# Turning the plain-head probabilities of batches 2 and 3 by transposing DMAs, in a fused windowed attention and two-layer MLP kernel

## The chip, the cores and the metric

The kernel runs on one core of one Trainium2 chip. The metric is the device time in microseconds (us) of one execution, taken as the median of several runs. Lower is better.

## The reference, cut to what matters

The inputs `q`, `k`, `v` are 8 batches x 8 heads x 576 positions x 64 features in float32. Heads 0 to 3 ("plain") look at the last 32 positions; heads 4 to 7 ("dilated", or "strided") look at every fourth of the last 128 positions. The attention result, seen as 4608 rows of 512, goes through a two-layer MLP with a SiLU between the layers.

```python
scores = scale * np.matmul(q, k.transpose(0, 1, 3, 2))
rel = pos[:, None] - pos[None, :]
mask_plain = (rel >= 0) & (rel < window)                                   # window = 32, heads 0..3
mask_dil = (rel >= 0) & (rel < window * dilation) & (rel % dilation == 0)  # dilation = 4, heads 4..7
scores = np.where(masks[None], scores, -1000000000.0)
scores = scores - np.max(scores, axis=-1, keepdims=True)
attn = np.exp(scores)
attn = attn / (np.sum(attn, axis=-1, keepdims=True) + 1e-09)
attn_out = np.matmul(attn, v)                 # 8 x 8 x 576 x 64
x = attn_out.transpose(0, 2, 1, 3).reshape(4608, 512)
h = x @ w_in                                  # 512 -> 2048
out = (h * (1.0 / (1.0 + np.exp(-h)))) @ w_out    # 2048 -> 512
```

## The kernel before, in words

The kernel works batch by batch. For each batch b there are 16 steps of layer one (`layer1`, one step for each of 16 groups of 128 hidden features; eight matmuls on TensorE and one SiLU on ScalarE a step) and then layer two (`layer2`, 16 or 20 steps of four matmuls of 128x512; every four steps end one tile of output rows, which VectorE copies out of PSUM and SyncE's queue stores). While TensorE does the MLP of batch b, the attention of the batches b+1 and b+2 is put between its steps. Nothing is scheduled automatically: the order of each engine's instructions is the order in which the Python code issues them. `plan_of(b)` writes a table from step numbers to calls (`at(step, function, ...)`), and `plan(s)` issues the calls of step s just ahead of that step's matmuls. Steps 0 to 15 belong to layer one, steps 16 and up to layer two; in layer two of batch 1 the steps run to 35.

The attention of one batch b comes in two halves, z = 0 (plain heads) and z = 1 (strided heads), each half in two parts hi = 0, 1, and each part goes through the same chain:

- `load_rows(b)` (lines 123 to 144) or `load_qk(b)`: GpSimd's queue loads q and k into a tile `nat`; `load_v(b)` loads v into `vw`, and `shift_*` copy parts of `vw` to other partitions.
- `cross(b, z)` (lines 146 to 159): two transposing DMAs on SyncE's queue for each half, out of `nat` into the tile `plain` (z = 0, line 152) or `strided` (z = 1, lines 158 and 159). Batch 3 is the first that is transposed so; batches 1 and 2 use TensorE (`transpose`).
- `scores(b, z)`: TensorE computes blocks of scores, VectorE adds the mask and takes maxima. `exps(b, z, hi)`: ScalarE's exponentials, with the sums.
- `normal(b, z, hi)` (lines 565 to 578): VectorE takes reciprocals of the sums and writes the normalised probabilities `pn` in float16, 8 or 10 blocks of 64 columns.
- The probabilities then have to be transposed, from `pn` to a tile `ptT`, which can be done in two ways. `turn` (line 585) lets TensorE transpose 4 or 5 blocks of 128x128 a part into PSUM, and `turned` (line 593) lets VectorE or ScalarE copy them to SBUF. `turn_by_dma` (lines 595 to 602) issues one transposing DMA on SyncE's queue, SBUF to SBUF, and needs neither TensorE nor the copy.
- `values(b, z)` (lines 627 and 691): TensorE multiplies by v. `finish(b, z, copies)` (lines 704, 696, 698): the copies of the result out of PSUM into `xT`, the input of layer one, by VectorE alone or, with `both`, half by VectorE and half by ScalarE.

In the kernel before, batches 0 to 2 and the plain half of batch 3 are turned by TensorE; the strided half of batch 3 and all of batches 4 to 7 by DMA. The helper `later` issues normalisation, turn, values and finish for batch 2 (both halves, in layer two of batch 1) and for the plain half of batch 3 (in layer one of batch 2, steps 0, 4 and 6).

SyncE's queue is in order: an instruction that waits holds up what stands behind it. In layer two of batch 1 it holds, in this order: the first two output tiles' stores, the third store, `cross(4, 0)` and `cross(4, 1)` at step 28, and the fourth and fifth store. GpSimd's queue holds the loads of batch 4 (`load_rows(4)`, from step 17), and at step 0 of batch 2 `load_v(4)` and the strided rows of batch 5, which start once `values(2, 1)` has set the old `vw` free.

PSUM has two tiles of the pool `big` for the matmuls of the MLP and four tiles of the pool `ps`, which scores, turns and values use in turn. `pn` and `ptT` have four buffers each.

Of the kernel before, what the change touches and what calls it, by code (L numbers as in the profile page):

```python
# [29 lines left out]
def kernel(  # L30
# [9 lines left out]
    nc = tc.nc  # L40
# [754 lines left out]
    def transposes(at, b, z, step):  # L795
        for which in (1, 0):
            at(step, transpose, b, z, which, both)

    def later(at, b, z, steps, copies=(nc.vector.tensor_copy, nc.vector.tensor_copy)):

        for hi in (0, 1):
            if steps[hi] is not None:
                at(steps[hi], normal, b, z, hi)
        for hi in (0, 1):
            at(steps[2], turn, b, z, hi)
        for hi in (0, 1):
            at(steps[2], turned, b, z, hi, copies[hi])
        at(steps[3], values, b, z)
        at(steps[3], finish, b, z, copies)

    def plan_of(b):
        ev = {}

        def at(s, fn, *args):
            ev.setdefault(s, []).append((fn, args))

        def all_exps(b, z):
            for hi in (0, 1):
                at(16, exps, b, z, hi)

        if b == 0:

            at(-16, normal, 0, 1, 1)
            at(-15, shift_class, 0, dve, 1, 2)
            at(-14, normal, 0, 0, 1)
            at(-8, turn, 0, 1, 1)
            at(-8, turned, 0, 1, 1, act)
            at(-4, turn, 0, 0, 1)
            at(-4, turned, 0, 0, 1)
            at(-4, values0, 1, 1)  # L830
            at(-4, last_values, 0, 1, (1,))
            at(-4, finish0, 1, 1)
            at(-4, last_finish, 0, 1, 1)
            at(-2, values0, 0, 1)
            at(-2, last_values, 0, 0, (1,))
            at(-2, finish0, 0, 1, both)
            at(-2, last_finish, 0, 0, 1)
            at(-2, clear_short, 1, nc.vector)
            at(-2, load_v, 1)
            for c in (2, 3):  # L840
                at(-2, load_w_out, c)
            at(-2, load_qk, 2)
            transposes(at, 1, 1, 2)
            at(8, scores, 1, 1)
            for hi in (0, 1):
                at(8, shift, 1, 1, hi)
            for which in (1, 0):
                at(18, transpose, 1, 0, which, (dve, dve) if which else (act, act))
            at(20, normal, 1, 1, 0)
            at(20, scores, 1, 0)  # L850
            at(14, shift_v, 1, nc.sync.dma_start)
            at(18, load_rows, 3)
            at(18, load_v, 2)
            all_exps(1, 1)
            for hi in (0, 1):
                at(20, exps, 1, 0, hi)
            for n, z, hi in ((20, 1, 1), (26, 0, 0), (28, 0, 1)):
                at(n, normal, 1, z, hi)
            for n, z, copies in ((27, 1, (dve, dve)), (30, 0, both)):
                for hi in (0, 1):  # L860
                    at(n, turn, 1, z, hi)
                for hi in (0, 1):
                    at(n, turned, 1, z, hi, copies[hi])
                at(n + 1 + z, values, 1, z)
                at(n + 1 + z, finish, 1, z, both)
        elif b == 1:
            transposes(at, 2, 0, 3)
            transposes(at, 2, 1, 11)
            at(2, shift_v, 2, nc.sync.dma_start)
            for z in (0, 1):  # L870
                at(2, cross, 3, z)
                at(28, cross, 4, z)
            at(9, scores, 2, 0)
            for hi in (0, 1):
                at(12, shift, 2, 0, hi)
            at(17, load_v, 3)
            at(17, nc.gpsimd.tensor_copy, latch, qTs[1][:, 1, S - 1 : S])
            at(17, load_rows, 4)
            at(14, scores, 2, 1)
            all_exps(2, 0)  # L880
            all_exps(2, 1)
            for hi in (0, 1):
                at(19, normal, 2, 0, hi)
            at(21, scores, 3, 0)
            at(21, exps, 3, 0, 0)
            at(21, exps, 3, 0, 1)
            later(at, 2, 0, (None, None, 27, 28))
            later(at, 2, 1, (29, 31, 33, 34))
        else:
            if b + 2 < B:  # L890
                at(0, load_v, b + 2)
                if b + 3 < B:
                    at(0, load_rows, b + 3, (1, 0))
                if b + 3 < B:
                    at(12, cross, b + 3, 0)
                if b > 2:
                    at(12, cross, b + 2, 1)
            if b + 1 < B:
                at(1 if b == 2 else 0, shift_plain, b + 1, dve, 0, NM)
                at(12, shift_class, b + 1, dve, 0, 2)  # L900
                at(12, shift_over, b + 1, dve)
                if b == 2:
                    later(at, 3, 0, (0, 0, 4, 6))
                else:
                    at(6, values, b + 1, 0)
                    at(6, finish, b + 1, 0)
                x = {2: 13, 3: 12}.get(b, 11)
                at(x, scores, b + 1, 1)
                at(x, shift, b + 1, 1, 1)
                all_exps(b + 1, 1)  # L910
            if b + 2 < B:
                at(18 if b == 2 else 17, scores, b + 2, 0)
                for hi in (0, 1):
                    at(18, exps, b + 2, 0, hi)
            if b + 1 < B:
                for hi in (0, 1):
                    at(22 + hi, normal, b + 1, 1, hi)
                    at(22 + hi, turn_by_dma, b + 1, 1, hi)
                at(29, values, b + 1, 1)
                at(29, finish, b + 1, 1)  # L920
            if b + 2 < B:
                for hi in (0, 1):
                    at(27 + hi, normal, b + 2, 0, hi)
                    at(27 + hi, turn_by_dma, b + 2, 0, hi)

        def plan(s):
            for fn, args in ev.pop(s, ()):
                fn(*args)

        return plan  # L930
# [49 lines left out]
    for b in range(B):  # L980
        plan = plan_of(b)
        if b == 0:
            for x in range(NFF):
                plan(2 * x - NFF)
                plan(2 * x + 1 - NFF)
                layer1_part(2 * x % NFF, 2 * x // NFF, first[x] if x < 4 else None)
        else:
            for f in range(NFF):
                plan(f)
                layer1(b, f)  # L990
        if b == 0:
            layer2_first(plan)
        else:
            layer2(b, plan)
        for s in range(NFF, 3 * NFF):
            plan(s)
# [30 lines left out]
```

## Time and profile before

| what | value |
|---|---|
| time before, median of 3 runs | 308.5 us (307.78 to 308.84) |
| the profiled execution: its time | 307.98 us |
| the profiled execution: span of its instructions | 306.1 us |
| granted TensorE clock, mean | 0.989 |
| TensorE (PE) busy | 294.8 us, 96% |
| VectorE (DVE) busy | 178.2 us, 58% |
| ScalarE (ACT) busy | 187.5 us, 61% |
| TensorE transposes of probabilities, `turn`, plain half of batch 2 | 9 in 0.50 us, at 88.39 us |
| the same, plain half of batch 3 | 9 in 0.50 us, at 102.81 us |
| transposing DMAs of probabilities (18 in the run), issue to landing | 2.4 / 2.6 / 7.9 us (least, median, most) |

PE is TensorE's matmuls, DVE VectorE, ACT ScalarE, POOL GpSimd, SP SyncE; a name with a q (SPq, POOLq) is that engine's instruction queue, which issues DMAs. Times of instructions are microseconds from the start of the span. A line number with L is a line of the kernel. The profiled execution takes 1.88 us more than its span (307.98 against 306.1), and is itself 0.52 us below the median of the runs.

### The profile page before, as it was taken

Reading aid. Unit: us, or ns where it says so; the run is one execution under the profiler, and the core shown is the slowest. Engines: PE = TensorE matmul, PEld = TensorE weight load, DVE = VectorE, ACT = ScalarE, POOL = GpSimd, SP = SyncE. Lnnn points to the kernel's source line nnn. Section 1 sums busy time; section 2 is a strip of 40 time slices with the busy share of each in tenths; the row PEclk is TensorE's granted clock in tenths of the full one; section 3 lists DMA queues with packets and bytes.
Section 4 is the critical chain, followed back from the end, with each engine's and each line's share of the span. In section 5 each row is a group of like instructions: output and inputs, shape, how many; then the busy total and the mean of one; then the engine's idle time right before and its main releaser. Section 6 shows DMA issues by size and latency. Waiting matters only on the chain.

```text
span 306.1 us, 10365 instructions
## 1 busy us (share of the span) xinstructions
PE 294.8 (96%) x4466; PEld 189.2 (62%) x4466; DVE 178.2 (58%) x370; ACT 187.5 (61%) x556; POOL 92.3 (30%) x139
## 2 busy tenths in 40 slices
PE   5689999999999999999999999999999999999995
PEld 2557754677555875477644775467644775477544
DVE  6896579518797738943785447842885344620011
ACT  2676677676894559945792558945793558246200
POOL 8634544962473831086007610040000000000000
PEclk9689999999999999999999999999999999999999
DMA  8999999999999999599889995494035000400022
GB/s 106 179 213 203 174 197 218 170 197 182 164 156 191 170 189 103 135 141 176 108 154 176 194 113 105 130 177 82 4 77 144 36 2 12 135 36 2 9 94 71
DMA packets 104878, 39.21 MB, mean 128 GB/s; under 512 B 79568, under 2 KB 100048, under 8 KB 104832
## 3 DMA queue, kind: packets, MB, share of 16 engines
q0 software_dynamic: 63104, 18.88, 62.6%
q1 hardware_dynamic: 41584, 19.60, 30.3%
q8 instruction: 35, 0.57, 0.8%
q14 instruction: 11, 0.09, 0.1%
q10 hardware_dynamic: 144, 0.07, 0.1%
HBM read 37.75 MB, written 9.44 MB: 154 GB/s over the span
## 4 chain that ended last, share of the span: by engine, by line
PE 87%; DMA 7%; ACT 2%; DVE 1%; issue 1%; POOL 1%; POOLq 0%; SPq 0%
PE h L717 36%; PE o L782 33%; PE o L756 5%; PE h L737 4%; DMA w_in<-in_moe_w_in_dram 4%; PE x L627 3%; DMA nat<-in_q_dram 2%; PE s L379 1%; PE s L391 1%; ACT pe L560 1%; PE t L329 1%; PE pt L585 1%; DMA ptT<-pn 1%; POOL nat L168 1%; PE xs L691 1%
## 5 line engine op out<-in xcount | busy, mean ns | idle before, releaser
L725 ACT ACTIVATE gT<-h 128x576 f16<-128x576 f32 x112 | 72.9, 651 | 77.5 <-PE h L717 77.3
L782 PE MATMUL o<-w_out,gT 128*128 128x512 f16 (+1 forms) x528 | 114.1, 373 | 0.0
L717 PE MATMUL h<-xT,w_in 128*128 128x288 f16 x896 | 113.5, 286 | 0.0
L717 PEld LDWEIGHTS <-w_in 128*128 128x128 f16 x896 | 86.4, 98 | 23.3 <-DVE xT L704 0.3
L782 PEld LDWEIGHTS <-gT 128*128 128x128 f16 x528 | 50.7, 98 | 54.9
L560 ACT ACTIVATE pe<-ms,nm 128x64 f32<-128x64 f32 x178 | 59.1, 333 | 2.8 <-DVE nm L528 2.7
L766 DVE COPY ob<-o 128x512 f32<-128x512 f32 (+1 forms) x34 | 23.1, 681 | 45.9 <-PE o L782 44.9
L512 DVE SCALAR_TENSOR_TENSOR ms<-s,mask 128x512 f32<-128x512 f32 x28 | 19.2, 686 | 35.7 <-PE s L391 24.7
L560 ACT ACTIVATION_READ_ACCUMULATOR pe<-ms,nm 128x1 f32 x178 | 33.2, 187 | 0.0
L704 DVE CAST xT<-x 128x512 f16<-128x512 f32 x26 | 16.8, 685 | 21.2 <-PE xs L691 21.2
L177 POOL DMA_DIRECT2D vw<-in_v_dram x16 | 10.1, 634 | 61.4 <-PE xs L691 59.2
L576 DVE TENSOR_TENSOR pn<-pe,r 128x640 f16<-128x640 f32 (+2 forms) x32 | 25.3, 792 | 1.1
L528 DVE TENSOR_REDUCE nm<-ms 128x10 f32<-128x640 f32 (+1 forms) x28 | 22.0, 787 | 1.0
L737 PE MATMUL h<-xT,w_in 128*128 128x256 f16 (+1 forms) x128 | 16.9, 286 | 1.6 <-issue 0.9
L134 POOL DMA_DIRECT2D nat<-in_k_dram x20 | 15.2, 764 | 6.7 <-DMA vw<-in_v_dram 6.0
L134 POOL DMA_DIRECT2D nat<-in_q_dram x20 | 14.6, 749 | 6.3 <-DMA nat<-in_k_dram 4.0
L756 PE MATMUL o<-w_out,gT 128*128 128x512 f16 x64 | 15.2, 379 | 0.2 <-issue 0.2
L737 PEld LDWEIGHTS <-w_in 128*128 128x128 f16 x128 | 11.9, 98 | 5.4 <-issue 1.9
L744 ACT ACTIVATE gT<-h 128x512 f16<-128x512 f32 (+1 forms) x16 | 10.1, 652 | 6.3 <-PE h L737 6.1
L627 PEld LDWEIGHTS <-vw 64*64 64x64 f16 x896 | 8.4, 108 | 5.2 <-issue 5.2
L766 ACT COPY ob_last<-o 128x128 f32<-128x128 f32 x1 | 0.3, 266 | 17.0 <-DVE ob_last L766 17.0
L569 DVE TENSOR_REDUCE l<-pe 128x10 f32<-128x640 f32 (+2 forms) x12 | 9.6, 801 | 1.5 <-ACT pe L551 1.4
(101 smaller groups left out, 257.7 us busy)
## 6 DMA issues: line engine op xcount, KB each, us to landing
out_dram<-ob SPq DMA_DIRECT2D x35, 256.0 KB, 2.5
vw<-in_v_dram POOLq DMA_DIRECT2D x8, 288.0 KB, 8.4
vw<-in_v_dram POOLq DMA_DIRECT2D x16, 128.0 KB, 5.6
w_in<-in_moe_w_in_dram POOLq DMA_DIRECT2D x4, 512.0 KB, 12.5
w_out<-in_moe_w_out_dram POOLq DMA_DIRECT2D x4, 512.0 KB, 11.2
nat<-in_k_dram POOLq DMA_DIRECT2D x6, 256.0 KB, 6.8
nat<-in_q_dram POOLq DMA_DIRECT2D x6, 256.0 KB, 8.2
nat<-in_k_dram POOLq DMA_DIRECT2D x20, 72.0 KB, 7.1
```

The source lines that it names most:

```text
L134: nc.gpsimd.dma_start(out=f[:, 2 * (1 - which) + h // 2, 0 : ZR - 1, h % 2], in_=src[b, h].rearrange("(m p) d -> p m d", p=RT),)
L512: nc.vector.scalar_tensor_tensor(out=ms[:, 0:8].rearrange("p (n t) c -> p n (t c)", n=2), in0=s[hi].rearrange("p n t c -> p n (t c)"), sca ...
L528: nc.vector.tensor_reduce(out=nm[:, 0:w], in_=ms[:, 0:w], axis=AX.X, op=ALU.max, negate=True)
L560: nc.scalar.activation(pe[:, t, :], slot(t), AF.Exp, scale=1.0 if b else scale, bias=nm[:, t : t + 1], accum_out=l[:, t : t + 1],)
L576: nc.vector.tensor_tensor(pn[:, 0:w], a["pe", z, hi][:, 0:w], r[:, 0:w, None].broadcast_to([P, w, KB]), ALU.mult)
L627: nc.tensor.matmul(dst, w, p, start=True, stop=True)
L717: nc.tensor.matmul(h[:, half, 0:HS], w_in16[:, c, f * P : f * P + P], xT[:, c, half * HS : half * HS + HS], start=(c == 0), stop=(c == MC ...
L725: nc.scalar.activation(gT[:, f, s0 : s0 + S].rearrange("p (a c) -> p a c", a=2), h[:, :, 0:HS], AF.Silu)
L737: nc.tensor.matmul(h[:, i, 0 : c1 - c0], w_in16[:, c, (f + i) * P : (f + i + 1) * P], xT[:, c, c0:c1], start=(c == 0), stop=(c == MC - 1),)
L756: nc.tensor.matmul(o, gT[:, f, t * P : (t + 1) * P], w_out16[:, f, :], start=(f == 0), stop=(f == NFF - 1),)
L766: copy(ob, o)
L782: nc.tensor.matmul(o, gT[:, f, t * P : (t + 1) * P], w_out16[:, f, m0:m1], start=(f == 0), stop=(f == NFF - 1),)
```

## The change

The plain halves of batches 2 and 3 are turned by `turn_by_dma` and no longer by `turn` and `turned`. For batch 2 the DMAs are issued at step 19 of batch 1, right behind each part's `normal`. For batch 3 the normalisation moves from step 0 of batch 2 to step 34 of batch 1, where its two parts stand on VectorE's queue before and after the `finish` of batch 2's strided half, and each is followed by its DMA. That `finish` is now shared by VectorE and ScalarE (`both`). `values` and `finish` keep their steps (28 of batch 1 and 6 of batch 2). `cross(4, 1)` moves from step 28 to step 35, behind batch 3's two new DMAs on SyncE's queue; `cross(4, 0)` stays at step 28. The helper `later` goes; its other calls are written out at the steps that they had.

```diff
@@ in plan_of, b == 1
             at(2, shift_v, 2, nc.sync.dma_start)
             for z in (0, 1):
                 at(2, cross, 3, z)
-                at(28, cross, 4, z)
+            at(28, cross, 4, 0)
             at(9, scores, 2, 0)
...
             for hi in (0, 1):
                 at(19, normal, 2, 0, hi)
+                at(19, turn_by_dma, 2, 0, hi)
             at(21, scores, 3, 0)
             at(21, exps, 3, 0, 0)
             at(21, exps, 3, 0, 1)
-            later(at, 2, 0, (None, None, 27, 28))
-            later(at, 2, 1, (29, 31, 33, 34))
+            at(28, values, 2, 0)
+            at(28, finish, 2, 0)
+            for hi in (0, 1):
+                at(29 + 2 * hi, normal, 2, 1, hi)
+                at(33, turn, 2, 1, hi)
+            for hi in (0, 1):
+                at(33, turned, 2, 1, hi)
+            at(34, values, 2, 1)
+            at(34, normal, 3, 0, 0)
+            at(34, turn_by_dma, 3, 0, 0)
+            at(34, finish, 2, 1, both)
+            at(34, normal, 3, 0, 1)
+            at(34, turn_by_dma, 3, 0, 1)
+            at(35, cross, 4, 1)
@@ in plan_of, b >= 2
-                if b == 2:
-                    later(at, 3, 0, (0, 0, 4, 6))
-                else:
-                    at(6, values, b + 1, 0)
-                    at(6, finish, b + 1, 0)
+                at(6, values, b + 1, 0)
+                at(6, finish, b + 1, 0)
```

More of the change, by code (lines that the diff above doesn't have):

```diff
@@ L797, in transposes @@
             at(step, transpose, b, z, which, both)
[L799 to L809, printed above, removed]
     def plan_of(b):
```

## The prediction

> **What bounds the kernel now.** I read the page first, then the chain of waits in order of time, then SyncE's and VectorE's timelines around the edit, last the landings of single DMAs.
>
> The page says that TensorE is busy for 96% of the span, and that the chain that ended last lies on it for 87%:
>
> ```profile
> PE 294.8 (96%) x4466; PEld 189.2 (62%) x4466; DVE 178.2 (58%) x370; ACT 187.5 (61%) x556; POOL 92.3 (30%) x139
> PE 87%; DMA 7%; ACT 2%; DVE 1%; issue 1%; POOL 1%; POOLq 0%; SPq 0%
> ```
>
> The chain in order of time (start, length, what) shows how the edited stretch lies on it:
>
> ```profile
> 88.39 0.50 PE pt L585 x9
> 88.89 0.86 PE o L782 x4
> 89.75 0.61 PE x L627 x64
> ...
> 102.81 0.50 PE pt L585 x9
> 103.31 1.96 PE h L717 x16
> 105.27 0.61 PE x L627 x64
> ```
>
> Each piece begins where the last one ends, so TensorE has no idle time here. The two groups of L585 are the transposes that go; the two groups of L627 are the `values` that must then wait for a DMA. SyncE's queue in the same stretch, with the line at which the DMAs of batch 3 stand in its order:
>
> ```profile
> 77.35 3.86 SPq L158 DMA_TRANSPOSE strided<-nat  x1
> 81.31 2.14 SPq L159 DMA_TRANSPOSE strided<-nat  x1
> 85.31 5.53 SPq L767 DMA_DIRECT2D out_dram<-ob  x3
> 91.07 6.24 SPq L152 DMA_TRANSPOSE plain<-nat  x2
> 97.49 3.42 SPq L158 DMA_TRANSPOSE strided<-nat  x1
> 101.01 1.18 SPq L159 DMA_TRANSPOSE strided<-nat  x1
> ```
>
> The queue is free from 83.45 to 85.31, where the DMAs of batch 2 will be issued. It is held by `cross(4, 0)` from 91.07 to 97.31, and the DMAs of batch 3 stand behind that. VectorE writes the probabilities of batch 2's second part, and those of batch 3, here:
>
> ```profile
> 83.85 0.82 DVE L576 TENSOR_TENSOR pn<-pe,r 128x640 f16<-128x640 f32 x1
> ...
> 99.97 0.69 DVE L576 TENSOR_TENSOR pn<-pe,r 128x512 f16<-128x512 f32 x1
> ...
> 101.03 0.83 DVE L576 TENSOR_TENSOR pn<-pe,r 128x640 f16<-128x640 f32 x1
> ```
>
> The last view is the landing of a transposing DMA of probabilities: all 18 of them (least, median, most), and then the one issued at 163.0 alone:
>
> ```profile
> DMA to landing us min/median/max: 2.4/2.6/7.9
> ...
> DMA to landing us min/median/max: 5.6/5.6/5.6
> ```
>
> The second is issued 0.7 us after GpSimd begins to load v and rows for a later batch (162.30); the same place in two other batches gives 7.9 (issued at 130.12, loads from 129.45) and 5.8 (199.24, loads from 198.57). Without such loads it is 2.4 to 2.7, once 3.2 and once 3.3. That spread decides this case.
>
> **What goes from TensorE.** Twice nine transposes, 0.50 us each time by the chain, 56 ns a transpose. TensorE has no gap on either side, so what goes from it shortens the chain: 1.00 us in all. No other matmul goes, so this is the most that the change can give. [...] The chain's 56 ns decide, and I take 1.00.
>
> **What goes from VectorE.** Two pairs of copies out of PSUM, 0.81 us at 88.76 and 0.80 at 103.36. VectorE is not on the chain here, so I count nothing for them; they make it earlier by 0.81 before `finish` of batch 2.
>
> **Batch 2's two DMAs, step 19.** The first part's `pn` is written by 82.6, the queue is free at 83.45, and an issue takes 1.2 us (the least of the 18): 83.5 to 84.7. The second part's `pn` ends at 84.67, so its DMA is issued at 84.8 and done issuing at 86.0. `values(2, 0)` comes at 89.75 less the 0.50 that has gone, 89.25. That leaves 4.45 us for the landing. The nearest row is the store that SyncE issues at 85.31 in the same traffic; it landed after 2.7 us, and the q and k rows that GpSimd issues between 81.4 and 86 landed after 3.0 to 3.5. By those the data are there at 87.5 to 88.3, and nothing waits. The far ends are 2.4 and 7.9, so the wait lies between nothing and 3.45 us; I take nothing. The first store is pushed from 85.31 to 86.1; its buffer is one of five and nobody waits for it.
>
> **Batch 3's normalisation, step 34.** Its instructions cost VectorE 1.05 us (part 0, from 99.54 to 100.6) and 1.28 us (part 1, to 101.9) as before; what moves is their place. The copies after the turn of batch 2's strided half end at 96.06 less 0.5, so part 0 runs to 96.6, while TensorE is still in `values(2, 1)` (which ends at 97.06 less 0.5). VectorE's half of `finish`, half of the 1.55 us that it now takes alone from 96.99 to 98.54, runs to 97.4; ScalarE, idle from 95.2 to 99.9, does the other half at the same time. Layer one of batch 2 reads `xT` from 98.4 on: nothing waits. Part 1 then runs to 98.7, and behind it stands the copy of the last output tile, which frees the PSUM buffer that the second step of layer one needs at 99.4. It now ends at 99.62 and would end at 98.7 + 0.69 = 99.4. So between nothing and 0.2 us are lost; I take nothing.
>
> **Batch 3's two DMAs.** Ahead of them on SyncE's queue stand `cross(4, 0)`, to 97.3 (0.5 earlier if its start moves with TensorE, at 96.8), and a store of 0.3 to 0.5 us. So the first is issued at about 97.7 and the second, whose `pn` is there at 98.7, at about 99.0. `values(3, 0)` comes at 105.27 less 1.00, 104.27. That leaves 5.3 us. GpSimd's loads begin at 96.97 less 0.5, ahead of both. By the quiet rows (2.6) the data are there at 101.6; by the loaded rows at 104.6 (5.6), 104.8 (5.8) and 106.9 (7.9): a wait between nothing and 2.6 us. The rows that have SyncE's own traffic of this very stretch are a strided transpose issued at 97.49, which landed after 8.7 us but moves over three times the data, and stores at 102.28 and 102.75 with 6.8 and 8.0, which stood behind both strided transposes. In the changed order those come after the turns. So I take a landing below the loaded rows, 3 to 5 us, and no wait, but only by 0.3 to 2.3 us.
>
> **`cross(4, 1)` moved to step 35.** Two issues, 3.42 and 1.18 us, move from 97.49 to about 100.3, and the fifth store behind them from 102.75 to about 105.5. The strided scores of batch 4 are needed in layer one of batch 3, after 144 us; the next thing on the queue is `cross(5, 0)` at 115.29. It costs nothing, and the cover is some 10 us.
>
> **Sum.** Profiled execution 307.98, less 0.50, less 0.50, and nothing added: 306.98. It lies 0.52 below the median of the runs (308.5), so the same 1.00 off the median gives 307.5 us, 0.32% less. A measurement of this kernel can tell about 0.3%, 0.93 us, from no change, so even the full gain hardly clears that.
>
> **The rivals.**
>
> *Late batch 3 (slower).* The two new DMAs are issued behind `cross(4, 0)` and in the middle of GpSimd's loads, and `values(3, 0)` holds all of TensorE's queue until the second one lands. If `cross(4, 0)` ends a microsecond later, because batch 2's turns have slowed the rows that it transposes, the second DMA is issued at 100; with 7.9 us it lands at 107.9, 3.6 us late. With 7.9 alone it is 2.6 late. Taking 2.8 in the middle, 308.5 - 1.0 + 2.8 = 310.3 us. It decides from a landing of 5.3 us on, and makes the kernel slower by more than 0.3% from about 7.2. For it: three of three turns issued beside GpSimd's loads took 5.6 to 7.9. Against it: those loads come in bursts, and the DMA is at 1.20 of its share from 96 to 104 us against 1.24 from 163 to 169. [...]
>
> *Short wait.* The same wait, but of 0.3 to 1.5 us (landing 5.6 to 6.8): most of the gain is given back, 307.8 to 309.0, middle 308.3. No change that can be measured.
>
> *Late batch 2.* The second turn of batch 2 takes 5.4 us, like the store issued at 88.87, or up to 7.9: it lands at 90.2 to 92.7 against 89.25, 1.0 to 3.4 us late, and the time is 308.5 to 310.9. Against it are the rows of 2.7 and 3.5 from the same moment.
>
> That the change does not do what it says can be excluded: both `turn`s are TensorE instructions, and they are gone.
>
> **How the numbers follow.** In time 0.42, short wait 0.18, late batch 3 0.28, late batch 2 0.12. In time gives 307.5, itself 306.9 to 308.0 by the spread of the runs. Of its 0.42, I put 0.32 at more than 0.3% faster, and 0.10 within, as the gain is so near the bound. Short wait is within. Of late batch 2 half is within and half slower, late batch 3 is slower: faster 0.32, same 0.34, slower 0.34. The range goes from 306.9 to the middle of the late case, 310.3; beyond it is about half of that case.
>
> **What would show it.** L585 must have 18 matmuls fewer and L600 four DMAs more. In time: in the chain, L627 near 89.2 and 104.3 follows L782 and L717 with no gap, and both DMAs of each pair have landed before. Short wait or late: TensorE's loads of weights show an idle time before L627 put down to `ptT`, in the first or the second place, and the landing of the turn just ahead of it is over 4.4 or 5.3 us. Wrong altogether: a new wait of TensorE in any other place, or a gain over 1.1 us, since I see only 1.00 on the chain.

## The result and the profile after

The changed kernel takes 316.49 us (median of 4 runs, 315.91 to 317.72) against 308.67 us before (4 runs): a ratio of 1.0256, 95% interval 1.0233 to 1.0279. The forecast was 307.5 us, with a range to 310.3. The profiled execution takes 315.91 us; its span of 313.4 us is 7.3 us longer than before. Ratios, here and below, are of the fast runs alone and medians of all runs, so where a kernel had a slow run (three of the versions below) its median lies above what its ratio says.

The page after. Eighteen matmuls fewer, and still TensorE's share of the span falls; in the chain by lines the transposing DMAs of probabilities rise from 1% to 5%. In the row of the granted clock, the 15th of 40 slices shows a 6. The profile of before has a 6 and an 8 in that row too, but in its second and third slice, at the start of the kernel; so the mean of 0.989 is the same in both profiles and shows nothing of it:

```profile
PE 298.5 (95%) x4448; PEld 191.3 (61%) x4448; DVE 177.4 (57%) x364; ACT 188.1 (60%) x558; POOL 91.7 (29%) x139
...
PEclk9999999999999969999999999999999999999999
...
PE h L717 35%; PE o L782 31%; DMA ptT<-pn 5%; PE h L737 5%; PE o L756 5%; PE x L627 3%; DMA nat<-in_q_dram 2%; PE s L391 2%; PE s L379 2%; ACT pe L560 1%; PE pt L585 1%; PE t L329 1%; PE xs L691 1%; POOL nat L168 1%; DVE pn L576 1%
```

The chain of waits in order of time (start, length, what) shows both places. Where the transposes stood, the chain now leaves TensorE, goes through a DMA, and comes back at `values` (L627):

```profile
84.96 5.06 DMA ptT<-pn
90.02 0.04 issue
90.06 0.68 PE x L627 x63
...
99.27 1.11 PE h L717 x10
100.38 9.13 DMA ptT<-pn
109.51 0.04 issue
109.56 1.04 PE x L627 x32
110.59 0.11 PE xs L691 x4
110.70 9.13 PE h L717 x56
```

The last line matters too: the 56 matmuls of layer one behind the second wait take 9.13 us; before they took 6.97, as these lines of the chain before show:

```profile
90.43 4.42 PE o L782 x20
...
105.95 6.97 PE h L717 x56
112.92 0.61 PE s L391 x64
```

The stretches of 2 us around the wait (busy time of PE first, then PEld, DVE, ACT, POOL; granted clock, DMA share and GB/s last) show TensorE idle, and then at half its clock:

```profile
106.00:108.00 2.00, 0.00 (x0) 0.00 (x0) 0.00 (x0) 0.00 (x0) 0.69 (x1) 1.00 1.75 153
108.00:110.00 2.00, 0.45 (x33) 0.44 (x36) 0.00 (x0) 0.00 (x0) 0.00 (x0) 0.57 1.37 133
110.00:112.00 2.00, 2.00 (x60) 1.48 (x53) 1.40 (x4) 0.00 (x0) 0.72 (x1) 0.50 1.36 179
112.00:114.00 2.00, 2.00 (x11) 1.25 (x9) 1.25 (x4) 0.65 (x1) 0.67 (x1) 0.50 1.57 161
114.00:116.00 2.00, 2.00 (x14) 1.42 (x13) 0.00 (x0) 0.70 (x2) 0.91 (x3) 0.73 1.95 145
```

SyncE's queue after. The four new DMAs (L600) are issued where they were expected, within 1.4 us; it is their landing that is late:

```profile
82.90 3.26 SPq L600 DMA_TRANSPOSE ptT<-pn  x2
86.25 4.00 SPq L767 DMA_DIRECT2D out_dram<-ob  x3
90.49 6.89 SPq L152 DMA_TRANSPOSE plain<-nat  x2
97.47 0.54 SPq L767 DMA_DIRECT2D out_dram<-ob  x1
98.11 3.57 SPq L600 DMA_TRANSPOSE ptT<-pn  x2
101.85 7.63 SPq L158 DMA_TRANSPOSE strided<-nat  x1
```

The ledger (what each place adds to the span) comes from comparing the starts of the same work in the two chains. At 82.3 the changed kernel is 0.10 us ahead. The 20 matmuls behind `values(2, 0)` start at 90.81, 0.38 later than before, though 0.50 of transposes are gone: a wait of 0.98. The 56 behind `values(3, 0)` start at 110.70, 4.75 later, with another 0.50 gone: 4.87 lost. Of these TensorE is idle for 0.48 and 3.76; the other 0.63 are the products themselves, which are split by the wait and run at the lower clock. The scores behind those start 6.91 later (119.83 for 112.92): 2.16 more, the slow matmuls. To the end of the chain only 0.07 is added, and 0.3 behind it. So 0.98 + 4.87 + 2.16 + 0.07 + 0.3, less 1.00 and 0.10, make the 7.3 us. The half clock lasts from 108.3 to 115.1 us. TensorE works from 109.56 on, and half of these 5.5 us, 2.8, is my estimate of what the clock costs; 2.16 and 0.63 add up to the same.

### The profile page after: what moved, and what is told of

The parts are those of the page before. It is cut to its first block, busy times and chain, and to the rows that moved or that the text cites. A ratio compares the mean times of both kernels' runs of the same rounds, so it can differ in the third digit from the quotient of the medians.

```text
span 313.4 us, 10336 instructions
## 1 busy us (share of the span) xinstructions
PE 298.5 (95%) x4448; PEld 191.3 (61%) x4448; DVE 177.4 (57%) x364; ACT 188.1 (60%) x558; POOL 91.7 (29%) x139
## 4 chain that ended last, share of the span: by engine, by line
PE 86%; DMA 8%; ACT 2%; DVE 1%; issue 1%; POOL 1%; POOLq 0%; SPq 0%
PE h L717 35%; PE o L782 31%; DMA ptT<-pn 5%; PE h L737 5%; PE o L756 5%; PE x L627 3%; DMA nat<-in_q_dram 2%; PE s L391 2%; PE s L379 2%; ACT pe L560 1%; PE pt L585 1%; PE t L329 1%; PE xs L691 1%; POOL nat L168 1%; DVE pn L576 1%
## 5 line engine op out<-in xcount | busy, mean ns | idle before, releaser
L717 PE MATMUL h<-xT,w_in 128*128 128x288 f16 x896 | 115.5, 290 | 0.0
L717 PEld LDWEIGHTS <-w_in 128*128 128x128 f16 x896 | 87.4, 99 | 24.5 <-DVE xT L704 0.3
L627 PE MATMUL x<-ptT,vw 64*64 64x32 f16 x896 | 10.7, 189 | 5.1 <-DMA ptT<-pn 5.0
L627 PEld LDWEIGHTS <-vw 64*64 64x64 f16 x896 | 9.1, 111 | 10.3 <-issue 10.3
L737 PEld LDWEIGHTS <-w_in 128*128 128x128 f16 x128 | 12.0, 98 | 4.4 <-issue 1.4
```

The lines of the kernel that those rows point to most:

```text
L627: nc.tensor.matmul(dst, w, p, start=True, stop=True)
L717: nc.tensor.matmul(h[:, half, 0:HS], w_in16[:, c, f * P : f * P + P], xT[:, c, half * HS : half * HS + HS], start=(c == 0), stop=(c == MC ...
L737: nc.tensor.matmul(h[:, i, 0 : c1 - c0], w_in16[:, c, (f + i) * P : (f + i + 1) * P], xT[:, c, c0:c1], start=(c == 0), stop=(c == MC - 1),)
```

## The experiments

Theory A says that the new DMAs land late because GpSimd's loads run beside them, each pair for itself; that TensorE then waits; and that the longer wait costs it its clock. Its rivals are B (only both pairs together are too much) and C (SyncE's own queue, ahead of the turns or behind them, makes them late).

### One pair at a time

Batch 2 alone: batch 3's `normal`, `turn`, `turned`, `finish` and `cross(4, 1)` go back to their places.

```diff
+            at(28, cross, 4, 1)
...
-            at(34, normal, 3, 0, 0)
-            at(34, turn_by_dma, 3, 0, 0)
...
-            at(35, cross, 4, 1)
```

> Only batch 2's plain half is turned by DMA; batch 3's plain half and the order of the batch 4 transposes are as before the change. Theory A (each pair of new DMAs lands late for itself, because GpSimd's loads run beside it): a wait of about 1.0 us at values(2,0) against 0.50 us of transposes saved, so about 0.4 us slower than before, 309.1 us. Theory B (batch 2's DMAs are harmless by themselves; what costs is the crowd that both pairs make together): no wait over 0.3 us, 308.2 to 308.5 us.

Measured 309.06 us, ratio 1.0012 (0.9986 to 1.0037). The profile has a wait of 1.4 us at values(2,0), with a landing of 5.7 us, so these DMAs are late without the other pair, and B is out for them. Whether GpSimd's loads are the reason this run can't say. The net is within what the runs can tell.

Batch 3 alone: `turn` and `turned` of batch 2's plain half at step 27 again, no DMA at step 19.

> Only batch 3's plain half is turned by DMA, with the rest of that part of the change; batch 2's plain half is turned by TensorE as before. Theory A: the second DMA of batch 3 still lands about 9 us after its issue, TensorE still waits 4 to 5 us at values(3,0) and its granted clock drops behind it: about 315 us. Theory B (batch 2's DMAs pushed the transposes of batch 4's q and k, and with them batch 3's DMAs): the wait shrinks to under 1.5 us, the clock stays, 308 to 309.5 us.

Measured 315.50 us, ratio 1.0206 (1.0156 to 1.0256): nearly the whole loss, so B is out here as well. The second DMA lands 8.85 us after its issue, and the matmuls behind it are slow:

```profile
101.34 8.85 DMA ptT<-pn
110.19 0.04 issue
...
111.38 9.40 PE h L717 x56
```

### The wait filled with work

`fill(20)` issues 20 matmuls of 128x512 on a spare PSUM tile, ahead of `values(3, 0)`; nobody reads their result.

```diff
+                if b == 2:
+                    at(6, fill, 20)
```

> The changed kernel with 20 matmuls of 128x512 on a spare PSUM tile ahead of values(3,0), some 4.3 us of work whose result nobody reads, in the place of the wait. Theory A (2.2 us of the loss are a clock that drops to half because TensorE stood idle for 4 us): the landing stays where it is, the granted clock stays at 1.0 behind it, the 56 matmuls of layer one behind values(3,0) take 7.0 us and not 9.1, and the time is about 2.1 us below the changed kernel's, 314.3 us. Rival (those matmuls are slow for another reason, such as the DMA traffic): they stay at 9.1 us and the time at 316.5 us or above.

Measured 313.33 us, ratio 1.0161 (1.0106 to 1.0216) against the changed kernel's 1.0256. The DMA lands as late as it did, but TensorE has something to do meanwhile, and the 56 matmuls are back at 6.97 us:

```profile
100.75 9.09 DMA ptT<-pn
109.84 0.04 issue
109.88 0.68 PE x L627 x63
110.56 0.06 PE xs L691 x8
110.62 6.97 PE h L717 x56
```

Its granted clock reads 1.00 in every stretch from 104 to 114 us. So the 2.16 us are a clock that fell while TensorE stood idle, and not the DMA traffic, which is nearly the same: 171 and 161 GB/s from 110 to 114 us here, 179 and 161 in the changed kernel. No length of a wait that brings it comes out of the traces. In the changed kernel the clock falls 2.5 us after the last matmul ahead of the wait, and reads 0.50 for about 6.8 us. Behind waits of 1.65 us (batch 4's plain q, k last; it ends at 122.36) and 2.48 us (batch 2 alone, rows held; it ends at 121.23) it is 0.83 from 120 to 130 us and 0.66 from 120 to 125, while in another run below (loads and values(2,0) later) a wait of 2.64 us leaves it at 1.00 from 105 to 120. So here no single length of a wait decides, and one of 1.65 us was followed by a lower clock too.

### What makes the landings late

First, GpSimd's loads at step 0 of batch 2 left out, so that old data are used in their place.

```diff
-                at(0, load_v, b + 2)
+                if b > 2:
+                    at(0, load_v, b + 2)
-                if b + 3 < B:
+                if b + 3 < B and b > 2:
                     at(0, load_rows, b + 3, (1, 0))
```

> The changed kernel without the loads that GpSimd issues at step 0 of batch 2: the v of batch 4 and the strided and plain q, k of batch 5 are not loaded (old data is used in their place). Everything else keeps its order. Theory A (GpSimd's loads slow the turns of batch 3): the second DMA lands within 2.6 to 3.5 us, TensorE does not wait at values(3,0), the clock stays at 1.0, about 309 us in all (308.67 less 1.0 plus the 1.0 us wait of batch 2). Theory C (SyncE's own queue, the transposes of batch 4 before and behind the turns, slows them): the landing stays over 6 us and the time over 313 us.

One run: 309.67 us, and `values(3, 0)` waits for nothing. The second DMA is issued at 102.86, and the products that read it run from 106.72 to 107.41 without a gap, so it lands within some 4 us. That is theory A. The time is nearer to 310 than to 309; this profile has a wait of 1.5 us at values(2,1) that nothing it shows ends (see below).

Then the plain q, k of batch 4 transposed behind batch 3's DMAs as well, which leaves only stores ahead of them on SyncE's queue.

```diff
-            at(28, cross, 4, 0)
...
+            at(35, cross, 4, 0)
             at(35, cross, 4, 1)
```

> The changed kernel with the plain q, k of batch 4 transposed behind batch 3's two new DMAs as well (step 35 and not 28), so that nothing but stores stands ahead of those on SyncE's queue. Theory A (GpSimd's loads at step 0 of batch 2 are what slows the turns): the DMAs are issued at about 96.7 and 98.8 us, 1.5 us earlier than in the changed kernel, the first lands before the loads get going (within 4 us), the second still takes over 6 us; the wait at values(3,0) shrinks by 1 to 3 us, the clock may hold, 311 to 315 us. Theory C (SyncE's own transposes ahead slow them): both land within 4 us, no wait there, about 309 us.

Measured 314.79 us, ratio 1.0228 (1.0178 to 1.0279). The second DMA of batch 3 was issued at 99.69 and still took 5.3 us: less than 9.1, far more than 2.6. So SyncE's queue may have a part. Whether it has one, and how large, the run can't say, since this DMA also started 0.7 us earlier, and so further ahead of the loads. The wait at values(3,0) is gone and the time is hardly better: now the scores of batch 3's strided half (1.4 us) and of batch 4 (1.6 us) wait, with no releaser in the profile, the clock is 0.83 in the two stretches from 120 to 130 us, behind the second of these waits, and values(3,1) waits for its DMA (0.6 us), as SyncE's queue comes to it only at 131.92.

I then tried to start the loads later by putting them at step 4; the second of these two runs also has values(2,0) at step 30 and not 28.

```diff
-                at(0, load_v, b + 2)
+                at(4 if b == 2 else 0, load_v, b + 2)
...
-                    at(0, load_rows, b + 3, (1, 0))
+                    at(4 if b == 2 else 0, load_rows, b + 3, (1, 0))
```

> The changed kernel with the loads of batch 4's v and batch 5's strided and plain q, k issued at step 4 and not 0 of batch 2, some 4 us later, nothing left out. Theory A: batch 3's second DMA lands within 4 us, before the loads run, no wait at values(3,0), the clock holds; the wait of about 1 us at values(2,0) stays, so about 308.7 us. What could be late instead: the transposes of batch 5's plain q, k stand ahead of batch 3's strided turns on SyncE's queue and wait for those loads, which would show as a wait of TensorE at values(3,1), up to 2 us. Theory C: the landing stays at 7 to 9 us, about 316 us.

> As the last one, and values(2,0) at step 30 and not 28. If the two causes are the landing of batch 2's second DMA 1 us after its need, and GpSimd's loads beside batch 3's, nothing waits any more and the whole 1.0 us of transposes is won: 307.7 us, 0.3% under the kernel before. If a wait at values(3,1) takes their place, 308.5 to 310 us.

Measured 315.36 (ratio 1.0218, 1.0176 to 1.026) and 315.84 us (1.0228, 1.0189 to 1.0266), with landings of 9.2 and 8.9 us. Both miss their point: the loads were not later. GpSimd's timeline in the first of them has the load right behind the first matmuls of values(2,1), as ever, because a step only orders a queue, and nothing on GpSimd's queue waits for steps of TensorE:

```profile
97.77 0.62 POOL L177 DMA_DIRECT2D vw<-in_v_dram  x1 [7.16 <-PE x L627]
```

So the next two hold GpSimd by data: it copies one column of the turned tile ahead of its loads (here `load_v(4)` and `load_rows(5)`).

```diff
+    def hold(b):
+        nc.gpsimd.tensor_copy(latch, att(b)["pt", 0, 1][:, 0, 0:1])
...
+            if b == 2:
+                at(0, hold, 3)
```

> The changed kernel, and GpSimd copies one element of batch 3's second turned tile ahead of its loads at step 0 of batch 2, so that these really start only when that DMA has landed (moving their step did not hold them, since GpSimd's queue waits for nothing else). Theory A: the second DMA of batch 3 lands within 4 us of its issue and values(3,0) waits for nothing; the wait of about 1 us at values(2,0) stays; 308.7 us, unless the loads, now some 5 us later, make something behind them late (values(3,1) or the transposes of batch 5), then 309 to 312 us. Rival (SyncE's own traffic slows the turn): it lands after 6 us or more, 315 us.

Measured 311.04 us, ratio 1.0091 (1.006 to 1.0123). GpSimd now waits for the turn, the second DMA lands after 2.7 us instead of 9.1, and values(3,0) follows layer one without a gap. GpSimd's timeline, the landing, and the chain:

```profile
104.33 0.19 POOL L800 COPY latch<-ptT 128x1 f16<-128x1 f16 x1 [13.93 <-DMA ptT<-pn]
```

```profile
DMA to landing us min/median/max: 2.7/2.7/2.7
```

```profile
99.83 5.88 PE h L717 x48
105.71 0.61 PE x L627 x64
106.32 0.20 PE xs L691 x8
106.52 6.97 PE h L717 x56
```

SyncE's queue holds the same instructions in the same order, so for batch 3 theory A is shown: without the loads beside it the DMA is not late. It isn't shown that the loads alone would make 9.1 us of it, since no run has batch 3's turns beside the loads without SyncE's q, k transposes near. The kernel stays slower than before: values(2,0) and values(3,1) wait, 0.7 and 0.9 us. And the same for batch 2, alone by DMA, with the rows of batch 4 held until its second DMA has landed:

```diff
-            at(17, load_rows, 4)
...
+            at(19, hold, 2)
+            at(19, load_rows, 4)
```

> Batch 2's plain half alone by DMA, and GpSimd holds the q, k rows of batch 4 in the same way until batch 2's second DMA has landed (they start near 88 and not 81 us). Theory A for batch 2 (those rows run beside its DMAs and make them land 1 us late): the landing falls to about 2.6 us, no wait at values(2,0), 308.0 to 308.5 us. Rival (the DMAs are late because they stand behind the transposes of batch 3 on SyncE's queue): the second still lands after 4.5 us or more and the wait stays.

The landing falls to 2.6 us and values(2,0) waits for nothing, as theory A has it; the rival (SyncE's queue ahead of the turns) is out. But the time is 316.39 us, ratio 1.0259 (1.0221 to 1.0298): the rows, issued from 88.19 us on (before: from 81.36), push SyncE's transposes behind them by 4.5 to 9.2 us (the first starts at 95.56 for 91.07, the last at 110.17 for 101.01). TensorE then waits in the scores of batch 4 (first two lines: 2.48 us that no semaphore explains) and for the next turns, and its clock is 0.66 in the stretches from 120 to 125 and from 135 to 140 us:

```profile
118.17 0.59 PE s L379 x61
118.76 2.48 issue
121.23 0.20 PE s L379 x3
...
132.78 2.66 DMA ptT<-pn
135.44 0.04 issue
135.49 1.04 PE x L627 x37
```

### Looking for a version that keeps the gain

With the products put where the DMAs have landed, values(2,0) at step 30 and values(3,0) at step 11 of batch 2:

> The changed kernel with the products with v put where the DMAs have landed: values(2,0) at step 30 and not 28 (1.7 us later), values(3,0) at step 11 and not 6 of batch 2 (4.9 us later). The landings stay what they are. If the loss is nothing but waits at those two places and the clock that follows, both waits go or shrink under 0.6 us each and the clock stays: 307.7 to 309 us. If the late landings hurt elsewhere too (layer one of batch 3, the scores of batch 3's strided half, PSUM tiles that come free later), new waits show and the time stays over 310 us.

Measured 316.98 us, ratio 1.028 (1.0257 to 1.0302). There is no wait left at values(2,0) or values(3,0), and the loss is as large: the scores of batch 3's strided half wait 3.95 us in the middle of their matmuls, the granted clock is 0.66 in the stretch from 115 to 120 us, and values(4,0) waits for a turn that lands after 8.7 us.

```profile
112.89 0.53 PE s L391 x54
113.42 3.95 issue
117.37 0.34 PE s L391 x10
```

Batch 3 alone with held loads, and both pairs with everything held at once (and both halves of batch 4's q, k transposed behind batch 3's turns):

> Batch 3's plain half alone by DMA, and GpSimd's loads held as in the last one. Theory A: neither values waits, 0.50 us of transposes are saved: 308.0 us, a ratio of 0.998. Rival: the held loads are missed later, 309 to 312 us.

> Both pairs by DMA, both groups of GpSimd's loads held, and both halves of batch 4's q, k transposed behind batch 3's DMAs. If waits for the new DMAs are all that the change costs, both go and the gain of 1.0 us shows: 307.4 us. If the DMA engines have no room for the work that is pushed back, TensorE waits later, for its scores, its probabilities or its instructions: over 310 us.

Measured 310.28 us, ratio 1.004 (1.0009 to 1.0072), and 316.03 us, ratio 1.0248 (1.0211 to 1.0285). In the second neither values(2,0) nor values(3,0) waits, but batch 3's second DMA still takes 5.1 us, with the held rows of batch 4 now beside it. The scores of batch 4 wait for 2.3 us with no releaser, values(3,1) for 3.6, and the clock is 0.66 in the stretch from 120 to 125 us, 0.88 from 130 to 135 and 0.50 from 135 to 140.

In the kernel with held loads, values(3,1) waited 0.9 us, as the transposes of batch 5's plain q, k stood on SyncE's queue ahead of its turns (they waited there 12.7 us for the held loads). The last two move those behind the turns:

```diff
-                    at(12, cross, b + 3, 0)
+                    at(29 if b == 2 else 12, cross, b + 3, 0)
```

> The changed kernel with GpSimd's loads held as before, and the transposes of batch 5's plain q, k moved from step 12 to step 29 of batch 2, behind the turns of batch 3's strided and batch 4's plain half on SyncE's queue. If the wait of 0.9 us at values(3,1) came from those transposes, which waited on SyncE's queue for the held loads, it goes, and the time falls by about 0.9 us against the kernel with held loads, to 309 to 310 us (the wait of 0.9 us at values(2,0) stays and eats the 1.0 us of transposes). If it came from elsewhere, nothing moves: 311 us.

> Batch 3's plain half alone by DMA, loads held, batch 5's plain q, k transposed at step 29. Nothing waits any more for a transposing DMA: 0.5 us under the kernel before, 308.1 us, a ratio of 0.998 (0.996 to 1.000). If TensorE still waits for its instructions or its clock behind the pushed loads, 309 to 311 us.

Measured 312.10 us, ratio 1.0088 (1.0053 to 1.0124), and 312.59 us, ratio 1.0088 (1.0058 to 1.0118). In the first the wait at values(3,1) did go, as expected, but the time did not fall: the same wait stands one batch further on, at values(4,1), whose turns stand on SyncE's queue behind the transposes for batches 5 and 6:

```profile
162.72 2.60 DMA ptT<-pn
165.32 0.04 issue
165.36 0.70 PE x L627 x63
```

No version beats the kernel before. The nearest, batch 2's pair alone, can't be told from it. Of the versions that removed a wait by moving or holding work, each got a new one elsewhere.

## Why the prediction was wrong

- *What goes from TensorE.* Right: 18 transposes fewer (4448 matmuls for 4466), and no other gain anywhere. VectorE's order at step 34 cost nothing that the ledger shows, and the PSUM tile was not late.
- *Batch 2's two DMAs.* Wrong in the landing taken. The second was issued at 84.96, as worked out (84.8), but landed after 5.06 us and not 2.7 to 3.5. The row that I took as nearest, the store issued at 85.31, was no measure: in the changed kernel the store behind the turns took 4.7 us. The rival "late batch 2" happened, at its low end (1.0 us).
- *Batch 3's two DMAs.* This is the step that decided, and it was wrong twice. The first issue took 2.17 us instead of 1.2, so the second came at 100.38 and not 99.0. And it landed after 9.13 us, beyond the largest of the 18 rows (7.9), where I took 3 to 5. I had three rows of turns issued beside GpSimd's loads, 5.6, 5.8 and 7.9, and argued myself below all three because SyncE's strided transposes would come later. The run with those loads held shows that the landing was late because of them: 2.7 us, with SyncE's transposes in the same order. The profile of before could have said which row was nearest. GpSimd's last load of v in each place landed after 8.7 us here (issued at 99.33), after 8.9 beside the turn of 7.9 (131.82) and after 6.5 beside that of 5.6 (164.94); and its rows here, issued from 100.5 to 104, took 10.0 to 11.2. I also misread a row of this very stretch: the second store was issued at 102.90, not 102.75, and landed after 9.1; the 8.0 is the median of the two stores.
- *The price of a wait.* Missing altogether, that is, put at nothing without a reason: the wait also halved the clock, to 0.50 from 108.3 to 115.1 us, which made 4.87 us into 7.0. My late rival had 2.6 to 3.6 us of wait and no clock.
- *The rivals as a set.* I gave late batch 2 and late batch 3 chances as if one excluded the other. Both come from GpSimd's loads, and they came together; with the clock they make the 7.3 us of the ledger, where the range ended 1.6 us above the kernel before. The late case, with the three rows that speak for it, was in the prediction at 0.28; that no more was given to it, and that its price stopped at 2.8 us, is what failed.
- *`cross(4, 1)` moved.* It was to cost nothing, and no wait in the changed kernel falls to its scores. Whether it slows the turn just ahead of it was not tested: no run has batch 3's DMAs beside the loads with `cross(4, 1)` at its old step. But the cover was smaller than said: its first issue took 7.63 us and not 3.42.
- What I did not see at all is that work moved in this stretch is missed later, though TensorE's chain before shows nothing of it: where a wait was removed by moving or holding work, a new one came up further on (3.95 us with the later values, 2.48 with batch 2's rows held, 2.3 with everything held).

## What to carry to other kernels

Price a DMA that replaces work of a busy engine by its landing in the traffic of its own place: rows of the same kind beside the same loads (here 5.6 to 7.9 us, and 9.1 came), not the quiet median (2.6) and not a store that happens to fall near. Rank such places by how late the loads themselves land. When an in-order engine may wait, ask also how long it will be idle, since the wait of nearly 4 us cost 2 us more in clock, and in two other runs waits of 1.65 and 2.48 us were followed by a lower clock as well (0.83 over 10 us, 0.66 over 5). And to delay a load, make its queue wait for data: moving it to a later step of another engine did nothing here.

## What the runs showed of the hardware that was not expected

TensorE stopped, behind the first 60 us of the span, for 0.4 to 3.95 us with no semaphore to wait for, always inside a run of small matmuls, in profiles where the order of work had moved (3.95 us at 113.42 with the later values, 2.48 us at 118.76 with batch 2's rows held, 1.5 us in the run without loads); the profile of before has nothing of the kind there. At the longest of them the clock falls as well (0.66 from 115 to 125 us; the 3.95 end at 117.37). In the stretch of the 2.48 us the DMA view has one transfer on a queue that it calls `instruction`, beside the two data queues:

```profile
q0 software_dynamic: 650, 0.24, 76.0%
q1 hardware_dynamic: 249, 0.45, 52.3%
q8 instruction: 1, 0.02, 2.5%
```

The view of the 3.95 us has one such transfer too, at 2.3%. That is all the views show of it: no run changes these transfers, so it is not shown what the matmuls waited for. That it could be instructions, as two of the expectations have it, was the author's guess.

Why a transpose of 160 KB takes 9 us beside GpSimd's loads stays open as well. The runs show that batch 3's second one landed after 9.1 us beside them and after 2.7 with them held, not how they make it late.
